# A fused pooled attention and mixture of attention experts: zero matmuls in groups of two, and a new order of all units

## The chip, the cores and the metric

The kernel runs on one core of a Trainium2 chip. The metric is device time in microseconds of one execution. The core has five engines with queues of their own: TensorE (PE, matrix products; PEld is its loading of the stationary operand), VectorE (DVE), ScalarE (ACT), GpSimd (POOL) and SyncE (SP, which here issues all DMA transfers). Each engine works through its own instructions in order and waits on semaphores for the others.

## The reference

Two stages, joined without a pause. With B = 8 batches, H = 8 heads, S = 576 rows, D = 64 columns and E = 4 experts:

```python
# stage 1: attention to keys and values averaged over windows of 8 rows
k_p = k.reshape(B, H, 72, 8, D).mean(axis=3)
v_p = v.reshape(B, H, 72, 8, D).mean(axis=3)
attn = softmax(q @ k_p.T / 8)                      # 576 x 72 for each head
x = (attn @ v_p).transpose(0, 2, 1, 3).reshape(B, S, 512)
# stage 2: each expert is a causal attention of one head; each row takes its two best
logits = x @ w_gate                                 # 4 per row
w = softmax of the two largest logits of a row
for e in range(4):
    a = softmax(causal((x @ wq[e]) @ (x @ wk[e]).T / 8))     # 576 x 576
    out += w[row, e] * (a @ (x @ wv[e]) @ wo[e])             # rows that chose e
```

The inputs q, k, v are 9.4 MB each in float32, the weights 2 MB together; the output is 9.4 MB.

## The kernel before

All matrix products are in bf16. A batch of 576 rows is cut into 512 main rows and 64 tail rows; the tails of two batches (b - 1 and b, for odd b) are put together and treated as one tile of 128 rows.

The work is cut into *units*, each a small Python generator that is run step by step. A unit's first step issues its TensorE work (or its load), the next step the evacuation of the PSUM tile by ScalarE or VectorE, a third step what follows. The string `ORDER` lists the steps of all units in the order in which they are issued: `2:kp` is the next step of unit `kp` of batch 2, `W:...` are units without a batch. `in_order` keeps each engine's instructions in the order in which they were issued, so `ORDER` fixes every engine's queue, the order of the loads on SP included. At the end of the kernel function a loop goes through it:

```python
for name in ORDER.split():
    if name not in parts:
        parts[name] = units[name]() or iter(())
    next(parts[name], None)
```

The units by name, for batch b:

- Loads, on SP: `lk`, `lq`, `lv` (1 MB each; in batch 0 halves `lka`, `lkb` and so on), the tails `lkt`, `lvt`, `lqt` (128 KB each), the weights `W:lq`, `W:lk`, `W:lv`, `W:lo`. All go through one DMA queue.
- `ks`, `vs`, `qc`: pairwise sums of the keys (ksum) and values (vsum), the cast of the queries (qbf), on GpSimd, for batch 0 on VectorE and ScalarE too. `kt`, `vt`, `qt`: the same for the tails (kts; vtp and vts; qtb).
- `kp`, `vp`: pooling by a matmul with a matrix of 1/8. `kp` is eight matmuls that read ksum and then four that read kts.
- `q0` to `q3`: transposes of the queries (qT). `s0` to `s3`: scores (sA), then the exponential on ScalarE (etA). `a0` to `a3`: attention times values (oA), then VectorE's division (x_tm). `x0` to `x3`: transposes of x (xT).
- `v0`, `v2`: the experts' values and the gate's logits (v_ps). `p0` to `p3`: the experts' queries and keys (p_ps), copied by ScalarE. `p0` and `p2` read wq, `p1` and `p3` read wk; `W:c0` to `W:c3` are ScalarE's casts of these weights. `g1` to `g6`: the gate on VectorE, GpSimd and ScalarE (g_lm, g_msk, g_w and so on).
- `c00`, `c01`, `c10`, `c11`, `c2`: the experts' scores in pieces (sB), exponential on ScalarE (etB, etC), GpSimd's causal mask. `o0`, `o1`: times values (oB). `t0`, `t1`: transposes (oT). `w0` to `w3`, `y0` to `y3`, `z0`, `z2`: output projection (y_ps), copy, store.
- For the pair of tails, under the odd batch: `qx`, `sx`, `ax`, `xx`, `pt`, `vx`, `h0`, `h1`, `hd`, `ox`, `tx`, `w4`, in the same sense.

The units `s*`, `c*`, `sx`, `h*` and `hd` have 64 rows in their contraction; all others have 72 or 128.

`W:h0` to `W:h9` are the function `busy`: four matmuls of 128x512 on a tile of zeros (`idle`, a view of `etd`), into a PSUM tile (idle_ps) that nobody reads. The tile comes from the pool `ps1`, which has two buffers and is shared with `q`, `x`, `t`, `kp`, `vp`, `p` and the `w` and `y` units; `s`, `a`, `v`, `c`, `o` and the like take turns in the three buffers of `ps2`.

Of the kernel before, what the change touches and what calls it, by code (L numbers as in the profile page):

```python
# [21 lines left out]
0:lkb 0:lqb 0:lkt W:h6 W:h9 0:lvb W:h5 0:qcb1 0:ksb W:h2 0:lqa 0:kt 0:lva 0:qcb0 0:qca0 W:h3 W:h8
0:qca1 0:lvt 0:q3 0:q3 0:q2 0:lka 0:vsb W:h0 1:lkt 0:vsa 0:kpb 1:kt 0:q2 0:q1 0:kpb 0:q1 0:q0 1:lk
0:ksa 0:s2 0:kpa 0:q0 0:vt 0:kpa 0:vp 0:s2 1:lq 0:s1 0:s3 1:ks 1:qc W:lv 1:lv 0:vp 0:a2 W:h4 0:s1
0:a1 W:lq 0:a2 0:s3 0:a3 0:s0 1:kp W:h1 0:a1 0:s0 0:a3 0:a0 W:h7 1:kp 1:lvt 1:q2 0:a0 1:q0 1:q2 1:q0
0:lqt 1:q3 1:q1 1:q3 1:vs 1:s2 1:lqt 1:q1 1:s3 0:x1 0:x1 1:vt W:cv 0:x2 1:s0 0:x3 0:x2 1:qt 0:x3
1:s2 1:s0 0:x0 1:s3 1:s1 0:x0 0:v2 0:v2 0:v0 1:vp W:lk W:c2 2:lq 0:v0 1:vp 0:p2 0:g1 1:s1 W:c0 2:lkt
0:p2 1:a1 0:g2 2:lvt 1:a3 1:qx 2:lk 1:a2 W:c3 0:p0 1:a1 1:qx 2:lv 1:a3 W:c1 0:g3 1:a0 1:a2 0:p3 0:p0
1:sx 0:g4 0:g5 2:qc 0:p1 1:a0 0:p3 1:sx 0:c11 3:lq 0:c10 1:x2 0:p1 3:lkt 1:x1 1:x2 0:c11 1:x1 2:lqt
0:c2 1:x0 1:x0 1:x3 0:c10 1:ax 1:x3 2:q3 3:lqt 2:q3 3:lk 1:p2 2:kt 0:g6 0:c11 0:c2 2:vt 3:lv 0:c00  # L30
0:c01 2:q2 1:p2 0:c2 2:q0 0:c10 2:ks 0:c01 1:ax 2:q2 1:v0 2:q1 4:lkt 2:q0 1:v0 1:xx 0:o1 1:v2 2:q1
0:c01 1:xx 3:lvt 2:kp 1:v2 0:c00 2:kp 1:pt 0:o1 2:s0 2:s2 2:vs 1:vx 1:pt 2:s0 0:c00 0:t1 1:vx 1:g1
2:s1 2:s3 2:vp 0:t1 1:g2 2:s2 0:o0 1:p0 2:s3 2:vp 2:s1 3:kt 2:a3 2:a1 0:o0 2:a2 1:p0 3:qt 1:p3 1:p3
1:p1 2:a3 4:lq 3:qc 4:lk 2:a2 2:a1 2:a0 1:p1 1:c10 3:qx 1:c10 3:q1 2:a0 3:q1 3:ks 1:h1 3:qx 1:hd
2:x3 2:x2 1:h1 2:x3 2:x2 1:h0 1:hd 2:x0 2:x1 2:x0 1:c11 1:c00 3:vs 3:vt 2:x1 1:c10 3:q0 3:q3 3:q0
1:g3 1:h0 2:v0 1:g4 3:q3 3:kp 1:c11 3:kp 1:c00 2:v2 0:t0 3:s3 2:v0 0:t0 1:c2 3:q2 2:v2 3:q2 2:p0
1:c2 4:kt 3:vp 3:sx 2:p0 1:c01 2:p1 2:g1 3:s3 3:sx 5:lq 1:c01 3:vp 3:a3 1:hd 2:p2 3:ax 2:p1 3:a3
1:g5 2:p2 3:s1 3:s0 4:qc 1:c2 3:ax 4:q0 4:q0 1:g6 4:lv 3:s1 1:ox 4:lvt 1:ox 4:q1 1:c00 4:q1 3:s0
3:s2 3:s2 2:c01 4:ks 2:g2 1:c01 2:c00 4:q2 4:q2 3:xx W:lo 3:xx 3:a1 4:lqt 2:c01 3:a1 4:kp 3:pt 4:kp
3:a2 3:a2 2:c00 5:lkt 4:q3 3:a0 3:pt 1:o0 5:lqt 4:s1 5:lvt 2:p3 4:q3 3:a0 1:c11 3:x0 4:s1 2:p3 4:s0  # L40
4:s0 4:s2 5:qc 3:x1 1:o0 5:lk 3:x0 3:x1 4:s3 4:s3 5:q2 4:vs 4:vt 5:q2 1:t0 1:o1 5:vt 3:x3 2:g3 1:t0
3:x3 2:c2 3:x2 4:vp 3:x2 6:lvt 4:vp 2:c2 3:p1 1:o1 3:v0 2:c00 4:s2 2:c01 6:lkt 3:v0 5:lv 3:p1 5:q3
1:t1 2:c10 3:h0 1:t1 W:co 4:a1 2:c10 3:p3 4:a0 5:qt 5:q3 5:kt 3:p3 3:p2 3:p2 4:a1 5:qx 4:a0 2:c11
4:a3 5:q1 5:qx 2:g4 3:p0 3:h0 5:q1 4:a2 2:c10 2:c11 2:g5 0:w1 4:a3 3:p0 7:lkt 4:a2 3:c10 3:c11 5:ks
0:w1 5:kp 3:c10 4:x0 4:x0 3:v2 3:c11 5:kp 4:x2 4:x2 0:w0 2:c11 6:lq 2:c2 0:w0 3:c2 3:v2 5:s1 5:vs
4:x3 3:c2 2:g6 4:x1 4:x3 4:x1 2:o0 3:vx 3:vx 5:s1 6:lv 2:o0 4:p2 6:qc 4:p2 0:w3 3:g1 0:w0 5:s2 6:vs
5:sx 3:hd 0:w3 5:q0 0:w3 5:q0 4:p1 5:s2 2:o1 5:vp 2:o1 5:vp 5:sx 4:v2 4:p1 3:c11 0:w2 4:v2 3:c10
3:hd 5:a2 1:w3 6:kt 5:a2 0:w2 5:s3 5:s0 2:t0 1:w3 5:ax 6:q1 2:t0 5:ax 4:p3 6:lk 0:w1 6:vt 7:lvt 5:s0
5:a0 7:kt 6:q1 5:a0 5:a1 3:g2 4:p3 4:p0 3:c2 5:xx 5:s3 3:h1 5:a1 4:p0 3:c00 2:t1 5:xx 5:a3 6:lqt
7:vt 2:t1 3:h1 5:pt 5:a3 3:c00 1:tx 6:ks 1:tx 3:hd 5:pt 4:c2 3:c01 7:lq 6:q0 6:q0 5:x2 4:c2 4:v0  # L50
3:c01 5:x3 5:x2 6:q3 5:x3 7:lk 4:c01 4:c00 6:q3 7:qc 4:c01 6:kp 6:vp 6:kp 6:vp 4:c00 1:w3 4:c2 2:w0
3:o1 4:v0 2:w0 5:x0 5:x1 5:x0 3:c00 6:s3 3:g3 6:s1 7:q2 5:x1 7:lv 6:s3 6:s1 4:g1 3:ox 7:lqt 3:g4
7:q2 5:p3 3:g5 6:a1 3:g6 5:p3 3:ox 0:w2 5:p2 7:ks 5:p2 4:c01 3:o1 6:a1 1:w4 4:g2 5:hd 6:s0 1:w4 5:hd
6:q2 6:q2 2:w0 6:s0 6:a3 7:kp 1:w4 7:kp 3:c01 7:q3 6:s2 7:q3 2:w2 6:s2 3:o0 1:w2 2:w2 6:a3 6:a0 1:w2
3:o0 6:a0 2:w1 6:a2 2:w1 5:p1 7:vs 1:w0 4:c11 2:w2 6:a2 5:p1 1:w0 7:s2 4:c11 7:s3 5:vx 7:qt 7:s3
7:vp 7:s2 5:vx 5:v0 6:x3 7:vp 6:x3 4:g3 4:c00 5:v0 6:x1 5:v2 6:x1 6:x0 4:c10 4:c10 4:c11 1:w2 7:q1
7:a2 6:x0 2:w3 7:q1 5:p0 1:w0 2:w3 1:w1 5:v2 7:a2 5:g1 5:p0 7:s1 4:g4 1:w1 5:h0 3:t1 4:c10 4:g5 6:x2
4:g6 3:t1 5:g2 4:o1 7:s1 6:x2 7:qx 7:qx 4:o1 5:hd 5:h0 6:p2 7:q0 7:q0 7:sx 5:h1 5:c10 3:t0 6:p2 5:g3
7:sx 3:t0 6:p0 5:h1 7:a1 6:p3 6:v2 5:c10 4:o0 6:p3 1:w1 6:p1 7:a1 5:c10 6:v2 6:p0 3:tx 5:g4 7:a3
7:s0 4:o0 5:g5 3:tx 5:c2 6:p1 7:s0 3:y1 3:w4 7:a3 2:w1 2:w3 3:y1 7:ax 5:c2 7:a0 7:ax 3:w4 3:w0 7:a0  # L60
6:v0 3:y1 3:w0 3:w3 5:c00 5:g6 3:w3 7:x2 6:v0 5:c2 5:c01 7:x1 7:x2 7:x3 3:w4 5:c11 5:c00 7:x1 6:c10
4:t0 7:x3 5:c01 4:t0 5:c00 6:g1 5:ox 3:w0 7:xx 6:c2 5:c11 6:g2 6:c10 5:c01 5:c11 7:xx 6:c00 6:c2
7:vx 5:ox 5:o0 6:g3 7:vx 4:t1 4:t1 7:x0 6:c00 5:o1 7:x0 6:c10 4:w2 4:w2 7:p1 7:v0 5:o1 4:w2 5:o0
3:w3 7:p1 7:p3 4:y0 7:v0 7:p3 6:c11 6:c01 4:y0 4:y1 5:tx 6:c11 7:v2 6:c2 5:tx 3:w2 6:c01 4:y1 6:g4
7:p2 7:v2 6:c11 3:w2 6:c01 6:g5 7:p2 7:p0 6:g6 7:g1 5:t0 7:p0 7:c11 7:c10 6:c00 7:c10 5:t1 5:t0
7:c10 4:w3 6:o1 3:w2 5:t1 4:w3 7:c11 6:o0 7:g2 4:y0 5:w4 7:pt 6:o1 5:w4 5:y2 7:g3 7:c01 7:pt 6:o0
7:g4 4:y1 5:y2 7:c01 6:t0 6:t0 7:c2 6:t1 7:c2 7:g5 7:c11 7:g6 6:t1 4:w3 7:c2 5:y0 7:c00 5:w4 5:y0
5:y1 7:c00 7:h1 6:y1 5:y2 7:c01 5:y1 6:y1 5:y0 5:y1 7:c00 7:o1 7:h1 6:y1 6:w0 6:w0 7:o0 6:w0 5:w3
7:o1 7:t1 7:h0 5:w3 7:o0 7:hd 7:hd 7:t1 7:t0 7:h0 6:y3 7:t0 5:w3 7:z2 6:y3 7:hd 7:ox 6:y3 6:w2 7:z2
7:z0 7:ox 6:w2 7:tx 6:w2 7:tx 7:z0 7:w4 7:w4 7:w4  # L70
"""


# [880 lines left out]
```

## Time and profile before

| | |
|---|---|
| runs shown, us | 178.42, 177.4, 179.2 (median 178.42) |
| the profiled execution, us | 179.14 |
| its span, first to last instruction, us | 177.4 |
| mean granted TensorE clock | 0.965 |
| TensorE busy | 164.7 us, 93% of the span |
| VectorE, ScalarE, GpSimd busy | 70%, 70%, 59% |
| read from and written to memory | 30.42 MB, 9.44 MB |
| matmuls on zeros | 40, in all 13.5 us busy |

Times within the profile count from the first instruction. In the timeline each row is a run of equal instructions: start, busy time, engine, line, operation, tiles, shapes, count, and in brackets the engine's idle time in front of it with what ended it. Nearly all instructions carry one line, L121, since a helper issues them; so they are told apart by tiles. A row for a stretch of time gives, after its length, the busy time of PE, PEld, DVE, ACT and POOL with their counts, then the granted clock, the DMA share and GB/s. In the row of the granted clock over 40 slices, 9 is full. Matmuls overlap at their ends, so that the time that a group of them takes is read from its start to the start of the next one.

### The profile page before, as it was taken

The page shows a single profiled execution, that of the slowest core. Times are in us where ns is not written, and L with a number is a line of the kernel's source. Part 1 is how long each engine was busy: PE and PEld are TensorE (multiplying, and loading weights), DVE is VectorE, ACT ScalarE, POOL GpSimd, SP SyncE. Part 2 cuts the span into 40 slices and gives each one's busy share as a digit, 9 for nine tenths or more (in the row PEclk, how much of TensorE's full clock was granted, in tenths as well). Part 3 has the DMA queues.
Part 4 walks back from the last instruction along what each step waited for, and adds up shares of the span by engine and source line. Part 5 has one row for each costly group of instructions (what it writes and reads, how often), then busy time and mean ns, then how long its engine had stood idle before and what let it go on. Part 6 is the DMA issues. An engine that isn't in the chain of part 4 may idle for free.

```text
span 177.4 us, 5397 instructions
## 1 busy us (share of the span) xinstructions
PE 164.7 (93%) x2172; PEld 105.3 (59%) x2172; DVE 124.2 (70%) x356; ACT 124.2 (70%) x172; POOL 103.9 (59%) x223
## 2 busy tenths in 40 slices
...
PEclk9978569999999999999999999999999999999997
DMA  4999999999799999799995999824040222165656
GB/s 154 314 313 308 346 304 200 337 276 312 185 259 328 305 336 343 168 240 270 276 318 133 321 318 361 235 61 177 6 181 0 91 92 76 46 236 164 256 183 234
DMA packets 38681, 40.20 MB, mean 227 GB/s; under 512 B 5632, under 2 KB 33792, under 8 KB 38656
## 3 DMA queue, kind: packets, MB, share of 16 engines
...
q8 instruction: 17, 0.28, 0.7%
...
HBM read 30.42 MB, written 9.44 MB: 225 GB/s over the span
## 4 chain that ended last, share of the span: by engine, by line
PE 68%; DMA 12%; SPq 7%; DVE 3%; ACT 3%; POOL 3%; issue 1%; DVEq 0%; POOLq 0%; ACTq 0%
PE p_ps L121 12%; PE v_ps L121 7%; SPq L121 7%; PE y_ps L121 7%; DMA ktail<-in_k_dram 5%; DMA qtail<-in_q_dram 5%; PE sB_ps L121 5%; PE oB_ps L121 4%; PE oA_ps L121 4%; PE sA_ps L121 4%; PE qT_ps L121 3%; PE xT_ps L121 3%; PE vp_ps L121 3%; PE idle_ps L121 2%; PE oBt_ps L121 2%; PE oT_ps L121 2%
## 5 line engine op out<-in xcount | busy, mean ns | idle before, releaser
L121 ACT ACTIVATE etA<-sA_ps 72x1024 bf16<-72x1024 f32 x32 | 31.6, 1020 | 14.2 <-PE sA_ps L121 13.9
L121 ACT ACTIVATE etB<-sB_ps 128x1024 bf16<-128x1024 f32 x32 | 31.8, 1031 | 2.8 <-PE sB_ps L121 2.3
L121 PE MATMUL p_ps<-xT,wqk 128*128 128x512 bf16 x128 | 32.6, 379 | 0.0
L121 POOL TENSOR_SCALAR_AFFINE_SELECT etB<-etB 128x256 bf16<-128x256 bf16 x48 | 18.6, 409 | 17.6 <-ACT etB L121 17.3
L121 ACT CAST qk<-p_ps 128x512 bf16<-128x512 f32 x32 | 18.6, 587 | 11.3 <-PE p_ps L121 11.2
L121 POOL TENSOR_TENSOR vsum<-vraw 128x512 bf16<-128x512 f32 (+1 forms) x16 | 18.9, 1203 | 9.8 <-DMA vraw<-in_v_dram 9.8
L121 DVE TENSOR_TENSOR x_tm<-oA_ps,rzA 128x512 bf16<-128x512 f32 x32 | 22.1, 692 | 1.1
L121 PEld LDWEIGHTS <-wqk 128*128 128x128 bf16 x192 | 14.6, 98 | 9.7 <-issue 0.4
L121 POOL TENSOR_TENSOR ksum<-kraw 128x512 bf16<-128x512 f32 x14 | 17.5, 1270 | 2.5 <-DMA kraw<-in_k_dram 2.5
L121 PE MATMUL y_ps<-wo_t,oT 128*128 128x512 bf16 x64 | 18.6, 380 | 0.0
L121 PE MATMUL v_ps<-wvg,xT 128*128 128x260 bf16 x128 | 16.8, 274 | 0.4 <-DVE xT L121 0.2
L121 PE MATMUL idle_ps<-etD 128*128 128x512 bf16 x40 | 13.5, 497 | 3.7 <-DVE qT L121 2.4
L121 DVE COPY xT<-xT_ps 128x512 bf16<-128x512 bf16 x32 | 12.6, 420 | 5.5 <-PE xT_ps L121 5.2
L121 DVE COPY qT<-qT_ps 128x512 bf16<-128x512 bf16 x32 | 13.1, 420 | 4.7 <-PE qT_ps L121 4.4
L121 ACT COPY ofin<-y_ps 128x512 f32<-128x512 f32 x20 | 11.7, 589 | 4.8 <-PE y_ps L121 3.5
L121 PEld LDWEIGHTS <-etA 72*128 72x128 bf16 x256 | 11.8, 102 | 5.3 <-issue 1.9
L121 POOL CAST qbf<-qraw 128x2048 bf16<-128x2048 f32 x7 | 13.2, 1892 | 1.4 <-DMA qraw<-in_q_dram 1.4
L121 PE MATMUL sB_ps<-qk 64*128 64x256 bf16 (+3 forms) x128 | 13.8, 300 | 0.0
L121 PEld LDWEIGHTS <-xT 128*128 128x128 bf16 x128 | 11.9, 97 | 3.2 <-DVE xT L121 0.5
L121 PE MATMUL oA_ps<-vp,etA 72*128 72x65 bf16 x256 | 13.3, 200 | 0.2 <-DVE vp L121 0.2
L121 PE MATMUL qT_ps<-ident,qbf 128*128 128x128 bf16 x128 | 12.1, 225 | 1.0 <-POOL qbf L121 0.6
L121 PEld LDWEIGHTS <-etB 128*128 128x128 bf16 x256 | 11.4, 97 | 1.6 <-POOL etB L121 0.2
(121 smaller groups left out, 331.7 us busy)
## 6 DMA issues: line engine op xcount, KB each, us to landing
...
```

The lines of the kernel that those rows point to most:

```text
L121: return tc.keep_in_program_order(fn(*args, **kwargs))
```

## The change

`busy` issues two matmuls in place of four, and there are 24 such units in place of ten, so 48 matmuls on zeros in place of 40. `ORDER` is another permutation: each other unit has as many steps as before.

```diff
     def busy():
         ps = ps1.tile([128, 512], FP32, name="idle_ps", tag="ps1")
-        for _ in range(4):
+        for _ in range(2):
             pe.matmul(out=ps[:], lhsT=idle[:, 0:128], rhs=idle, start=True, stop=True)
 
-    for n in range(10):
+    for n in range(24):
         units[f"W:h{n}"] = busy
```

`ORDER` has some fifty lines on either side; the sequences that follow from it on single engines are these. TensorE, the beginning (a unit stands where its TensorE work is issued; h is one group on zeros):

```text
before  h h h h h h 0:q3 0:q2 h 0:kpb 0:q1 0:q0 0:s2 0:kpa 0:vp 0:s1 0:s3 0:a2 h 0:a1 0:a3 0:s0
        1:kp h 0:a0 h 1:q2 1:q0 1:q3 1:q1 1:s2 1:s3 0:x1 0:x2 1:s0 0:x3 0:x0 1:s1 0:v2 0:v0 1:vp
        0:p2 1:a1 1:a3 1:qx 1:a2 0:p0 1:a0 0:p3
after   h h h h h h h 0:q1 h h h 0:q0 0:q3 h h 0:kpb h h 0:s3 0:kpa 0:q2 0:s0 0:s1 h h h 0:vp
        0:s2 h h 0:a0 0:a1 h 0:a2 1:kp 0:a3 h h h 1:q3 h 0:x0 1:s3 0:x1 1:q0 0:x2 0:x3 1:s0 1:q1
        0:v2 0:v0 1:q2 1:s1 1:s2 1:vp 0:p2 1:a3 1:a1 1:qx 1:a0 0:p0 1:a2 0:p3
```

TensorE, from there to the experts' first work on batch 2:

```text
before  1:sx 0:p1 0:c11 0:c10 1:x2 1:x1 0:c2 1:x0 1:x3 1:ax 2:q3 1:p2 0:c00 0:c01 2:q2 2:q0 1:v0
        2:q1 1:xx 0:o1 1:v2 2:kp 1:pt 2:s0 2:s2 1:vx 0:t1 2:s1 2:s3 2:vp 0:o0 1:p0 2:a3 2:a1 2:a2
        1:p3 1:p1 2:a0 1:c10 3:qx 3:q1 1:h1 1:hd 2:x3 2:x2 1:h0 2:x0 2:x1 1:c11 1:c00 3:q0 3:q3
        2:v0 3:kp 2:v2 0:t0 3:s3 1:c2 3:q2 2:p0 3:vp
after   1:sx 0:p1 1:x0 0:c10 0:c11 1:x3 1:x2 1:ax 0:c01 2:q0 1:x1 0:c00 0:c2 1:p2 1:xx 1:v0 2:q1
        2:q2 1:v2 2:kp 2:q3 0:o1 2:s0 1:pt 1:vx 2:s1 2:s3 2:s2 0:t1 2:vp 0:o0 1:p0 2:a0 2:a2 1:p3
        2:a1 1:p1 2:a3 3:qx 1:hd 1:h1 3:q1 1:c10 1:c00 2:x0 2:x1 1:h0 2:x3 2:x2 1:c11 3:kp 3:q3
        2:v0 3:q0 3:q2 1:c2 3:s3 2:v2 2:p0 0:t0 1:c01 3:sx 3:s1 3:vp
```

TensorE, the end:

```text
before  ... 6:o0 5:w4 7:pt 5:y2 7:c01 6:t0 7:c2 6:t1 5:y0 7:c00 5:y1 7:h1 6:y1 7:o1 6:w0 7:o0
        5:w3 7:t1 7:h0 7:hd 7:t0 6:y3 7:z2 7:ox 6:w2 7:z0 7:tx 7:w4
after   ... 5:w4 6:o0 5:y2 7:pt 7:c2 7:c00 6:t1 6:t0 7:c01 5:y0 5:y1 7:h1 6:y1 7:o1 6:w0 7:o0
        5:w3 7:t1 7:h0 7:hd 7:t0 6:y3 7:z2 7:ox 6:w2 7:z0 7:tx 7:w4
```

The loads on SP, the first 29 and 30:

```text
before  0:lkb 0:lqb 0:lkt 0:lvb 0:lqa 0:lva 0:lvt 0:lka 1:lkt 1:lk 1:lq W:lv 1:lv W:lq 1:lvt 0:lqt
        1:lqt W:lk 2:lq 2:lkt 2:lvt 2:lk 2:lv 3:lq 3:lkt 2:lqt 3:lqt 3:lk 3:lv
after   0:lvt 0:lqa 0:lkb 0:lqb 0:lkt 0:lka 0:lvb 0:lva 1:lkt 1:lk 1:lq W:lv 1:lvt 1:lv W:lq 1:lqt
        2:lkt 0:lqt W:lk 2:lq 2:lvt 2:lk 2:lv 3:lkt 3:lq 3:lqt 2:lqt 3:lk 3:lv 3:lvt
```

GpSimd, around batches 2 and 3 (masks named by their tile):

```text
before  ... ksum2 etB vsum2 etB g_lm g_msk kts3 qtb qbf3 ksum3 vsum3 vtp3 vts3 etB g_w ...
after   ... ksum2 etC etB g_G vsum2 etB qtb qbf3 g_lm g_msk ksum3 kts3 g_w g_d g_den etD vsum3 vtp3 vts3 ...
```

More of the change, by code (lines that the diff above doesn't have):

```diff
@@ L21 @@
 ORDER = """
[L22 to L70, printed above, removed]
+W:h21 W:h19 0:lvt W:h11 W:h12 0:lqa 0:qca1 0:lkb 0:lqb W:h16 0:lkt W:h1 W:h0 0:qca0 0:ksb 0:q1 W:h23
@@ new lines @@
+0:p2 W:c3 1:qt 1:a1 W:c1 1:qx 1:a3 1:qx 1:a0 0:p0 0:g2 1:a2 1:a0 2:lk 0:g3 0:p3 0:p0 0:p3 1:a1 0:g4
+2:lv 1:sx 2:qc 1:sx 0:p1 1:a2 3:lkt 1:x0 1:x0 0:p1 0:g5 0:c10 3:lq 0:c11 0:c10 2:vt 3:lqt 1:x3 1:x2
+1:ax 1:x3 0:c01 2:q0 0:c11 1:x2 1:x1 2:lqt 0:c10 1:ax 3:lk 0:c00 0:c11 0:c2 1:x1 1:p2 2:ks 0:c01
+2:q0 0:c2 1:xx 1:p2 0:c00 1:xx 1:v0 0:c2 0:c01 0:g6 2:q1 2:q2 2:q1 1:v2 2:q2 2:kp 2:q3 2:vs 1:v0
+2:kp 0:c00 0:o1 3:lv 2:q3 0:o1 2:s0 4:lvt 1:v2 1:pt 2:s0 1:vx 2:s1 1:vx 2:s3 2:s2 1:pt 1:g1 0:t1
+2:s1 2:vp 0:o0 0:t1 2:vp 2:s2 3:qt 2:s3 3:qc 1:p0 2:a0 2:a2 1:p3 0:o0 1:p0 2:a1 1:p1 2:a0 3:lvt 2:a2
@@ new lines @@
+1:p3 1:g2 2:a3 3:ks 3:qx 1:p1 4:lq 1:hd 2:a1 2:a3 1:h1 3:kt 1:g3 3:q1 1:hd 3:q1 3:qx 1:c10 1:g4
+1:c00 1:h1 2:x0 2:x0 1:hd 2:x1 1:h0 2:x3 1:c10 3:vs 3:vt 2:x1 1:c00 2:x2 1:c11 2:x3 3:kp 2:x2 3:kp
+3:q3 1:g5 2:v0 3:q0 3:q3 4:qc 1:c11 4:lk 3:q2 1:h0 4:lkt 2:v0 1:c2 3:s3 3:q0 2:v2 3:q2 2:p0 0:t0
+2:v2 5:lq 4:ks 1:c2 1:c01 0:t0 3:s3 3:sx 4:kt 4:lv 3:s1 2:p0 1:g6 4:vt 3:vp 3:vp 2:p2 1:c01 4:q0
+3:sx 3:a3 4:q0 2:g1 1:c00 3:s1 3:ax W:lo 2:p2 2:p1 4:q1 3:s0 3:a3 1:c2 2:p1 3:s0 3:s2 4:q1 3:ax 5:lk
+4:q2 1:ox 2:c00 2:c01 4:q2 1:c01 3:s2 5:lkt 2:c00 1:ox 5:qc 3:xx 3:a1 4:kp 3:a2 3:xx 1:c11 2:c01
```

37 lines of the change are left out of this document (added).

## The prediction

> **What bounds the kernel now.** I read the page first: span, granted clock and DMA in 40 slices.
>
> ```profile
> span 177.4 us, 5397 instructions
> ...
> PEclk9978569999999999999999999999999999999997
> DMA  4999999999799999799995999824040222165656
> ```
>
> The reader is to see that DMA is at its limit nearly throughout for 25 of the 40 slices (4.4 us each, to 111 us), and that the clock is below full only in slices 3 to 6. So there is a first regime in which loads come too late for TensorE, and a second in which TensorE alone is the bound. The chain of waits, in order of time, says where the first one ends:
>
> ```profile
> 34.22 1.04 ACT wqk L121 x2
> ...
> 44.12 8.79 DMA qtail<-in_q_dram
> ```
>
> This transfer, on the chain until 52.9 us, is the last load in it. So what TensorE does before that time is not worth its own length: it counts only by how much work is left when the last late transfer has been digested. GpSimd digests the loads; its timeline gives their arrivals, since an idle time that ended with a DMA ends at the landing:
>
> ```profile
> 21.73 1.89 POOL L121 CAST qbf<-qraw 128x2048 bf16<-128x2048 f32 x1 [0.51 <-DMA qraw<-in_q_dram]
> ...
> 43.24 2.50 POOL L121 TENSOR_TENSOR ksum<-kraw 128x512 bf16<-128x512 f32 x2 [0.67 <-DMA kraw<-in_k_dram]
> ...
> 49.56 0.22 POOL L121 TENSOR_TENSOR g_lm<-L,g_mx 128x20 f32<-128x20 f32 x1
> ...
> 51.55 0.46 POOL L121 TENSOR_TENSOR kts<-ktail 128x128 bf16<-128x128 f32 x1 [1.23 <-PE p_ps L121]
> 53.06 0.61 POOL L121 CAST qtb<-qtail 128x512 bf16<-128x512 f32 x1 [1.05 <-DMA qtail<-in_q_dram]
> 53.62 1.90 POOL L121 CAST qbf<-qraw 128x2048 bf16<-128x2048 f32 x1
> 55.79 2.52 POOL L121 TENSOR_TENSOR ksum<-kraw 128x512 bf16<-128x512 f32 x2 [0.27 <-DMA kraw<-in_k_dram]
> ```
>
> TensorE's own timeline, around the places that the change touches:
>
> ```profile
> 24.78 1.16 PE L121 MATMUL idle_ps<-etD 128*128 128x512 bf16 x4
> 25.78 0.61 PE L121 MATMUL qT_ps<-ident,qbf 128*128 128x128 bf16 x8
> ...
> 35.58 1.03 PE L121 MATMUL p_ps<-xT,wqk 128*128 128x512 bf16 x4
> ...
> 45.80 0.38 PE L121 MATMUL kpT_ps<-pm,ksum 128*128 128x64 bf16 x7 [0.21 <-POOL ksum L121]
> ...
> 54.53 0.40 PE L121 MATMUL qTt_ps<-ident,qtb 128*128 128x128 bf16 x4
> 55.57 0.40 PE L121 MATMUL qT_ps<-ident,qbf 128*128 128x128 bf16 x4 [0.64 <-POOL qbf L121]
> ...
> 58.58 0.62 PE L121 MATMUL qT_ps<-ident,qbf 128*128 128x128 bf16 x8
> 59.38 1.05 PE L121 MATMUL v_ps<-wvg,xT 128*128 128x260 bf16 x8 [0.17 <-ACT etX L121]
> 60.27 0.39 PE L121 MATMUL kpT_ps<-pm,ksum 128*128 128x64 bf16 x8
> 60.50 0.26 PE L121 MATMUL kpT_ps<-pm,kts 128*128 128x32 bf16 x4
> 60.61 1.05 PE L121 MATMUL v_ps<-wvg,xT 128*128 128x260 bf16 x8
> 61.50 0.38 PE L121 MATMUL oT_ps<-ident,o_sc 128*128 128x128 bf16 x4
> 61.82 0.39 PE L121 MATMUL sA_ps<-qT,kp 64*128 64x512 bf16 x2
> 62.04 0.38 PE L121 MATMUL sB_ps<-qk 64*128 64x256 bf16 x4
> 62.36 0.40 PE L121 MATMUL qT_ps<-ident,qbf 128*128 128x128 bf16 x4
> 62.59 0.59 PE L121 MATMUL p_ps<-xT,wqk 128*128 128x512 bf16 x2
> ```
>
> Matmuls overlap, so I take times from start to start. The row of 45.80 is 2:kp, waiting for batch 2's key sums; that of 55.57 is 3:q1, waiting for GpSimd's cast; both are the DMA regime showing through.
>
> **The change part by part.**
>
> *Eight more zero matmuls (48 for 40).* Four at half clock run from 24.78 to 25.78, partly after the clock has recovered, so about 0.25 us each; at half clock throughout it would be near 0.4 us. All 48 stand ahead of batch 0's value projection 0:v2, in the loading regime. Cost if uncovered: 8 x 0.25 = 2.0 us (0.2 to 0.4 each: 1.6 to 3.2). What covers them: TensorE waits for loads there anyway. I take zero.
>
> *The start.* Before, batch 1's queries are cast by 21.73 + 1.89 = 23.6, but TensorE begins them at 25.78 because zero groups of four stand in front. After, batch 0's attention outputs stand ahead of 1:kp, and three groups of two between 0:a3 and 1:q3. 1:kp needs GpSimd's ksum, done by 21.2 (GpSimd is idle for 0.51 us before 21.73) and, now behind it, kts (0.46, row of 51.55): 21.7. Then 0:a3 and six zero matmuls (1.5 to 2.4) lead to 1:q3 at 23.6 to 24.4, 1.4 to 2.2 us sooner. That doesn't hold: 0:p3 needs wk, whose cast on ScalarE (34.22, two casts in 1.04) released it at 35.58, and in the new load order batch 2's key tail stands in front of wk. That is a small transfer; I put wk at the old time to 1 us later. So 0:p3 comes between 34.8 and 35.9, against 35.58. I take no change.
>
> *2:kp.* The loads issued up to batch 2's keys are the same set in both orders (counted in ORDER), and DMA is at its limit throughout, so they land again at 43.2 and ksum ends at 43.24 + 2.50 = 45.7. The new order runs 2:kp before 2:q3 and 0:o1, which stood ahead of it: 0.22 + 0.61 = 0.83 us of work that is no longer done by then. TensorE waits here, and loses up to 0.83 us for the moment.
>
> *3:q1.* The transfers up to the later q tail of batches 2 and 3 are again the same set; it lands at 53.0, the cast ends at 53.62 + 1.90 = 55.5. Before, TensorE stood at 3:qx at 54.53 and waited 0.64 us and more; the 0.83 us of moved work now fills that wait. So 3:q1 at about 55.6 as before: the loss is given back.
>
> *3:kp.* This is where the new order decides. It moves 3:kp ahead of 3:q3, 2:v0 and 3:q0, and on GpSimd moves batch 3's key tail (kts) from before the casts (51.55) to behind ksum, with three small gate steps (0.22 each, 0.7) in front of ksum. Its bound: 55.5 + 0.7 + 2.52 + 0.46 = 59.2. Before the end of 3:kp the new order has done just what the old one had done by 58.58 (3:q0), and 3:kp itself, which is 12 small matmuls, 0.34 us (60.27 to 60.61). So it is late by 59.2 - (58.58 + 0.34) = 0.28 us. TensorE arrives sooner: from 55.57 to 58.58 the old order ran 3.0 us of small units; the new one has h1 and hd (55.57 to 58.58 holds them, 0.6 us) already behind it and 1:c10 (0.2) still to do, so 2.6 us, and 3:kp begins near 58.2. It waits some 0.8 us between its first eight and its last four matmuls. Without the wait it would end at 58.5 and be ahead by 0.4 us; with GpSimd 0.5 us later than reckoned, behind by 0.8. I take +0.28, from the row of the wait's releaser.
>
> *2:v0.* Before, it started 0.8 us after 3:q0 for 0.45 us of transposes, so it lost 0.33 us to late copies of xT. After, its transposes are older by a whole 3:kp. -0.33.
>
> *Switches between 64-row and 128-row work.* In the last four rows: oT before a 64-row unit takes 0.32 us (61.50 to 61.82), qT before other 128-row work 0.23 (62.36 to the next unit at 62.59); sA before another 64-row unit takes 0.22, sB before a 128-row unit 0.32. Each stretch of 64-row units thus costs 0.2 us. Counted in ORDER there were 52 such stretches, now 49; the three that go lie behind 2:v0, where nothing but TensorE is the bound. -0.6 us. It could be nothing if other waits fill the holes, and I see no way in which it costs.
>
> *The rest.* Every unit is there once in both; behind 60 us the new order permutes neighbours. The last eighteen units of TensorE, from 5:y1 to 7:w4, stand in the same sequence, and so do the stores. Tail: 0, bounded by 0.5 us either way from the order of 7:c01 and 7:c00 in front of it.
>
> Sum: 0.28 - 0.33 - 0.6 = -0.65 us. The profiled execution took 179.14 us, its span 177.4 us; the runs shown have a median of 178.42 us, 0.7 us under it. So 178.5 us against the profiled execution, and **177.8 us** as a median.
>
> **The clock.** The wait in 3:kp has a second price. Three stretches of 3.41 us at the start:
>
> ```profile
> 14.82:18.24 3.41, 2.13 (x22) 1.14 (x23) 1.94 (x5) 1.21 (x2) 1.20 (x3) 1.00 1.09 330
> 18.24:21.65 3.41, 3.20 (x30) 2.01 (x29) 1.45 (x5) 1.73 (x2) 2.49 (x2) 0.50 1.10 346
> 21.65:25.07 3.41, 3.41 (x27) 1.72 (x28) 1.74 (x5) 2.14 (x3) 1.89 (x1) 0.50 1.10 346
> ```
>
> In the first TensorE was busy for 2.13 of 3.41 us, 62%, and the granted clock (the column before the DMA share) was 0.50 in the next two. The Trainium skill, "TensorE: Matmul & The Clock Gate", Part 1 and the closing table, says that the clock falls after a whole idle window of some 3.4 us and tells the author to avoid gaps over about 3 us. By that rule a wait of 0.8 us would cost nothing beyond itself; the first row disagrees, as no gap there was near 3 us, and the measurement decides.
>
> **The rivals.**
>
> *Slower: the clock drops in the middle of the kernel.* Place: the wait in 3:kp (or that in 2:kp). It decides if the idle time in one window passes about 1.3 us (38% of 3.41, as in the first row). One window at half clock costs 1.7 us, two as in the trace 3.4 us: 179.5 to 181.2 us. For it: 0.8 us of expected idle time, and as much in front of it at 2:kp, are not far off. Against it: in a wait that falls across two windows neither is idle enough, and between 25 and 175 us the clock never fell in the trace of before, with the wait at 55 us in it. Chance 0.18. To the same side, at 0.08: the extra zero matmuls are not covered (0:p3 later than 36.5), 179.4 to 181 us.
>
> *Faster: the loading regime ends sooner.* If the later q tail and batch 3's keys land 1.5 us sooner, 3:q1 and the bound of 3:kp move by as much: 178.42 - 0.65 - 1.5 = 176.3 us. For it: the chain of before has a DMA on it as late as 52.9 us. Against: the same bytes stand in front of each late transfer, and DMA had no idle time to give. Chance 0.22.
>
> *The change does nothing:* the start is taken back and the switches fill other waits, 178.4 us. It lies inside the forecast's own range.
>
> **How the numbers follow.** The forecast, with its own range of 176.6 to 179.4 us (from the wait in 3:kp gone and the tail 0.5 us better, to the switches at nothing, that wait 0.5 us longer and the tail 0.5 worse), has 0.52. I call 1% (1.8 us) the least that a measurement tells from no change: faster is under 176.6, slower over 180.2. The faster rival lies mostly under its bound and a little of the forecast's lower side with it: 0.23. The slower ones at 0.26 lie mostly over theirs: 0.20. Within 1%: 0.57. The range that leaves out one in ten on each side is 175.9 to 180.5 us.
>
> **What would show it.** In the profile of the changed kernel: 0:p3 at 34.8 to 35.9; ksum of batch 2 again released by its DMA near 43.2 and 2:kp waiting for it; 3:q1 near 55.6 without a wait over 0.3 us; an idle time of about 0.8 us within 3:kp, ended by kts; granted clock 1.00 from 30 us on. If 2:kp or 3:kp come more than 1 us sooner, the claim that the same set of loads lands at the same time is wrong; if the clock falls after 30 us, the slower rival is right; if TensorE's work from 3:kp to the end isn't about 0.6 us shorter, the price of the switches is.

## The result and the profile after

| | before | after |
|---|---|---|
| time, us, median of 20 executions each | 178.43 (177.28 to 180.56) | 179.76 (178.53 to 181.51) |
| ratio to before | | 1.0071 [1.0042, 1.0099] |
| profiled execution, us, and its span | 179.14, 177.4 | 180.0, 178.3 |
| mean granted TensorE clock | 0.965 | 0.992 |
| TensorE busy | 164.7 us, 93% | 163.3 us, 92% |

The change costs 1.3 us where I forecast a gain of 0.65 us. The time is within 1% of before and within the range of 175.9 to 180.5 us, but it is on the other side of before, and outside the forecast's own 176.6 to 179.4 us. Ratios compare means without the few executions that lie over 1.5% above the fastest of their kernel, while medians are of all; two traces below, that without zeros and that of the late moves on GpSimd, are of such executions, and only their landings, their durations in the start and their wait at one place are read. The page of the changed kernel:

```profile
span 178.3 us, 5414 instructions
...
PEclk9999999999999999999999999999999999999996
DMA  3999998999999999969998997124050050443766
```

The clock row is full to the last slice, where before it fell in four slices. DMA is again at its limit for about 25 slices. So TensorE had, by this row, a better clock, it had less busy time, and it was later all the same: it waited more. The chain of waits, in order of time, has the later tails of the queries on it as before, and a stretch that before's did not need:

```profile
44.05 9.23 DMA qtail<-in_q_dram
...
105.95 1.28 POOL vsum L122
107.64 1.84 POOL qbf L122
```

GpSimd is on the chain at 106 to 109 us, 50 us behind the place where I had let the loading regime end. What TensorE waited for after 60 us, first before, then after (columns: waiting and releasing engine with tile, us in all, times, longest):

```profile
PE yt_ps L121 <- DVE oTt L121: 0.4, 1, 0.4
PE oT_ps L121 <- DVE o_sc L121: 0.2, 1, 0.2
```

```profile
PE oB_ps L122 <- POOL etB L122: 0.6, 1, 0.6
PE yt_ps L122 <- DVE oTt L122: 0.4, 1, 0.4
PE p_ps L122 <- ACT qk L122: 0.2, 1, 0.2
PE oT_ps L122 <- DVE o_sc L122: 0.2, 1, 0.2
```

Two waits are new: one of 0.6 us for a mask of GpSimd, one of 0.2 us for a copy of ScalarE. The first on TensorE, at 3:o1, and what GpSimd did before it:

```profile
109.97 0.60 PE L122 MATMUL y_ps<-wo_t,oT 128*128 128x512 bf16 x2
111.17 0.33 PE L122 MATMUL oB_ps<-vaug,etB 128*128 128x65 bf16 x5 [0.60 <-POOL etB L122]
```

```profile
100.25 2.50 POOL L122 TENSOR_TENSOR ksum<-kraw 128x512 bf16<-128x512 f32 x2 [1.95 <-DMA kraw<-in_k_dram]
...
104.72 2.50 POOL L122 TENSOR_TENSOR vsum<-vraw 128x512 bf16<-128x512 f32 x2
107.18 0.46 POOL L122 TENSOR_TENSOR kts<-ktail 128x128 bf16<-128x128 f32 x1
107.58 1.90 POOL L122 CAST qbf<-qraw 128x2048 bf16<-128x2048 f32 x1
109.43 0.77 POOL L122 TENSOR_SCALAR_AFFINE_SELECT etB<-etB 128x256 bf16<-128x256 bf16 x2
110.14 0.62 POOL L122 CAST qtb<-qtail 128x512 bf16<-128x512 f32 x1
110.70 0.77 POOL L122 TENSOR_SCALAR_AFFINE_SELECT etB<-etB 128x256 bf16<-128x256 bf16 x2
```

The reader is to see a chain without a hole: batch 6's keys land at 100.18, GpSimd sums them from 100.25 and works on to the masks of 3:c11 (109.43) and 3:c10 (the first of the two at 110.70), which 3:o1 needs. Their exponentials had long been done; in `ORDER` the masks stand behind the cast of batch 7's queries. In the kernel before the same three masks were done by 98.6 us, 11 us ahead of 3:o1, and 3:o1 started 0.43 us behind 2:w0 (y_ps), where the changed kernel has 1.20 us:

```profile
97.44 1.13 POOL L121 TENSOR_SCALAR_AFFINE_SELECT etB<-etB 128x256 bf16<-128x256 bf16 x3
```

```profile
109.19 0.59 PE L121 MATMUL y_ps<-wo_t,oT 128*128 128x512 bf16 x2
109.62 0.31 PE L121 MATMUL oB_ps<-vaug,etB 128*128 128x65 bf16 x5
```

To place the loss I use TensorE's *lag*: how much later it starts a unit than the kernel before had come to the same amount of work, both counted from the first instruction, matmuls on zeros left out. It is exact where both orders have done the same units; elsewhere it depends by some 0.2 us on how long each unit is taken to be. At such places the changed kernel is 0.70 us late (63.5 us of the kernel before), then 0.78 (106 us), 1.50 (118 us) and 1.59 (170 us). The jump is 3:o1.

### The profile page after: what moved, and what is told of

Same layout as the page of the kernel before. It is cut to its first block, busy times and chain, and to the rows that moved or that the text cites. A ratio compares the mean times of both kernels' runs of the same rounds, so it can differ in the third digit from the quotient of the medians.

```text
span 178.3 us, 5414 instructions
## 1 busy us (share of the span) xinstructions
PE 163.3 (92%) x2180; PEld 104.9 (59%) x2180; DVE 123.8 (69%) x356; ACT 124.6 (70%) x172; POOL 103.2 (58%) x223
## 4 chain that ended last, share of the span: by engine, by line
PE 50%; DMA 18%; SPq 10%; POOL 7%; ACT 5%; DVE 4%; issue 3%; DVEq 0%; POOLq 0%
PE p_ps L122 11%; SPq L122 10%; DMA qraw<-in_q_dram 7%; PE y_ps L122 6%; PE v_ps L122 6%; DMA qtail<-in_q_dram 5%; DMA wk_f<-in_moe_wk_dram 5%; PE oB_ps L122 4%; PE sB_ps L122 3%; POOL qbf L122 3%; PE sA_ps L122 3%; PE oA_ps L122 2%; PE oBt_ps L122 2%; PE xT_ps L122 2%; PE qT_ps L122 2%
## 5 line engine op out<-in xcount | busy, mean ns | idle before, releaser
L122 PE MATMUL idle_ps<-etD 128*128 128x512 bf16 x48 | 14.3, 422 | 4.2 <-DVE qT L122 2.2
L122 PE MATMUL sB_ps<-qk 64*128 64x512 bf16 (+3 forms) x128 | 13.5, 300 | 0.5 <-ACT etD L122 0.4
L122 PE MATMUL oB_ps<-vaug,etB 128*128 128x65 bf16 x256 | 12.4, 193 | 0.6 <-POOL etB L122 0.6
L122 PEld LDWEIGHTS <-etA 72*128 72x128 bf16 x256 | 10.6, 97 | 3.6 <-DVE vaug L122 0.2
```

Of the source, the lines that this page charges most:

```text
L122: return tc.keep_in_program_order(fn(*args, **kwargs))
```

## The experiments

Each is compared with the kernel before on the same chip; the ratio has its 95% interval. Where a diff shows `ORDER`, only the moved steps and their neighbours stand in it.

**1. The suspected masks alone.**

```diff
-... 3:h1 5:a3 4:c2 7:qc 1:tx 3:c01 3:c11 5:x2 7:qt ... 6:vp 3:c10 3:c00 ...
+... 3:h1 5:a3 4:c2 3:c11 3:c10 7:qc 1:tx 3:c01 5:x2 7:qt ... 6:vp 3:c00 ...
```

> The changed kernel with one difference: GpSimd's masks for 3:c11 and 3:c10 stand ahead of its cast of batch 7's queries (7:qc, 1.90 us), not behind that cast and the copy 7:qt. Theory (the order of GpSimd's queue costs 0.77 us at 3:o1): TensorE no longer waits at 3:o1 near 110 us, its work after that comes 0.6 to 0.8 us sooner, and the time is about 179.0 us, 0.35 to 0.45% under the changed kernel. Rival (another wait fills the hole, or the cast of batch 7's queries is then late for 7:q2): the time stays at 179.7 us.

Measured: 179.46 us, 1.0073 [1.0047, 1.0098]. TensorE no longer waits at 3:o1, but in the profiled execution it was 1.29 us late at 106 us already, so it had little to wait for. By time the theory fails here; experiments 9 and 10 come back to it.

**2. Two early tail loads put back**, and with them the GpSimd steps that read them, 1:vt and 2:kt.

```diff
-W:lv 1:lvt 1:lv ... W:lq W:h6 ... 1:lqt 2:lkt 1:qc 1:vt ... 2:lq W:h17 ... 2:kt 2:lvt ... 2:qc 1:sx
+W:lv 1:lv ... W:lq 1:lvt W:h6 ... 1:lqt 1:qc ... 2:lq 2:lkt W:h17 ... 1:vt ... 2:lvt ... 2:qc 2:kt 1:sx
```

> The changed kernel with two of the small tail loads put back where the kernel before had them: batch 2's key tail behind batch 2's queries, batch 1's value tail behind wq. Theory (in the loading regime everything that TensorE waits for comes late by the small loads in front of it, but batch 2's keys end the regime and have the same loads in front of them in all orders): wk and batch 2's queries land 1 to 2 us sooner than 35.0 and 39.2 us, 2:q0 loses its wait of 0.72 us, but 2:kp and 3:kp stay within 0.3 us of 45.8 and 59.4, so the time falls by no more than 0.5 us. Rival (the late loads at the start are what makes the changed kernel slower): the time falls by 1.0 to 1.3 us, to that of the kernel before.

Measured: 179.86 us, 1.0086 [1.0061, 1.0111]. wk and batch 2's queries landed at 34.2 and 37.7 us, 0.8 and 1.6 us sooner, and the lag at 36.5 us went from 0.50 to nothing. At 63.5 us it was 1.18: batch 3's keys landed at 56.6 us (56.1 in the changed kernel). What the start gains is not carried past those keys.

**3. The start and the rest exchanged.**

```diff
-ORDER: all of one kernel
+ORDER: one kernel's steps up to 1:a2 (or 1:sx) near 37 us, then the other's order for what is left
```

> The start of the changed kernel, all 24 groups of two matmuls on zeros and its loads included, up to the second half of 1:a2 near 37 us, and from there the order of the kernel before. Theory (the start costs little, since 2:kp and 3:kp wait for the same loads; the loss comes later): 178.4 to 178.9 us, as the kernel before. Rival (the eight more matmuls on zeros and the late wk make the loss): 179.5 to 179.8 us, as the changed kernel.

> The mirror of the run before: the start of the kernel before, with its ten groups of four matmuls on zeros and its loads, up to the first half of 1:sx near 37 us, and from there the order of the changed kernel. Theory (the loss comes after the start): 179.4 to 179.8 us, as the changed kernel. Rival (the loss is made in the start): 178.3 to 178.6 us, as the kernel before.

Measured: new start and old rest 178.24 us, 1.0006 [0.9973, 1.0039]; old start and new rest 179.08 us, 1.0053 [1.0013, 1.0093]. The new start, with its 48 matmuls on zeros, was 0.75 us late at 42 us and 0.19 us early from 58 us to the end. The loss lies behind 37 us.

**4. The same cut near 79 us.**

```diff
-ORDER: all of one kernel
+ORDER: one kernel's steps up to 5:q2 near 79 us, then the other's order for what is left
```

> The changed kernel up to 5:q2 near 79 us, and from there the order of the kernel before. Theory (half of the loss lies behind 80 us, in TensorE's waits for GpSimd's masks at 3:o1 and for PSUM tiles to be emptied, which took the place of the stretches of 64 rows that are gone): 178.8 to 179.2 us, and the time from the landing of batch 3's keys to the end of TensorE's work as in the kernel before plus 0.3 us. Rival (all of it lies in the loading regime, where loads land later): 179.5 to 179.8 us, as the changed kernel.

> The mirror: the kernel before up to 5:q2 near 79 us, with its ten groups of four matmuls on zeros, and from there the order of the changed kernel. Theory (half of the loss lies behind 80 us): 178.7 to 179.1 us, and the time from the landing of batch 3's keys to the end of TensorE's work 0.3 to 0.8 us longer than in the kernel before. Rival (all of it lies in the loading regime): 178.2 us, as the kernel before.

Measured: new order to 79 us and old behind it 178.88 us, 1.0041 [1.0011, 1.0071]; the mirror 180.16 us, 1.0121 [1.0075, 1.0167]. The mirror is not clean: its order asks for 5:kp sooner than the old loads bring batch 5's keys (82.3 us, 80.3 in the changed kernel), and TensorE waits 1.0 us there for GpSimd. But it has the same moral: an order of TensorE's units is only as good as the loads and the GpSimd queue that it was made with. And the first of the two has the old masks and no wait at 3:o1, and is still 0.1 to 0.7% slower than before: a part of the loss lies ahead of 79 us.

**5. No matmuls on zeros, and half as many again.**

```diff
-... W:h21 W:h19 0:lvt W:h11 W:h12 0:lqa ...
+... 0:lvt 0:lqa ...
```

```diff
-        for _ in range(2):
+        for _ in range(3):
             pe.matmul(out=ps[:], lhsT=idle[:, 0:128], rhs=idle, start=True, stop=True)
```

> The changed kernel with no matmuls on zeros at all; nothing else differs. Theory (their time is covered by waits for loads, and they keep the granted clock up in the start): TensorE is busy 14 us less, the granted clock falls to about half in the start, and the time is the same within 0.5 us if the loading regime covers that too, up to 1.5 us longer if it doesn't. Rival (the matmuls on zeros are on the path, 48 at 0.2 us and more): the time falls by over 1 us, to 178.6 us or less.

> The changed kernel with three matmuls on zeros in each of the 24 groups, so 72 for 48; nothing else differs. The 24 more take 24 x 0.22 = 5.3 us of TensorE at full clock, of which 14 x 0.22 = 3.1 us stand in front of the first queries; between 5 and 25 us TensorE was idle for 4.9 us in the profile of the changed kernel. Theory (covered): batch 0 and 1 come up to 2 us later at 25 us, but 2:kp and 3:kp wait for the same loads, so the time is the same within 0.5 us. Rival (on the path): up to 5 us longer.

Measured: without them 180.65 us, 1.0128 [1.0071, 1.0186]; with 72 of them 180.36 us, 1.0134 [1.0078, 1.019]. In the trace of the second the 24 more were covered: the lag was 0.86 us at 36.5 us and nothing at 63.5 us, under that of the changed kernel. Then TensorE came to 3:o1 early and waited 1.21 us for the same masks: lag 0.34 at 106 us, 1.45 at 110.5. By time the expectation of at most 0.5 us is missed: the ratio is 0.6% over the 1.0071 of the changed kernel, though the intervals overlap. Its trace loses another 0.65 us between 121 and 129 us, where a matmul of 7:vp waits 0.29 us for a copy of ScalarE; why, no run shows. The kernel without them is told of in the last section.

**6. GpSimd's order in the middle.**

```diff
-2:vp 2:s2 3:qt 2:s3 3:qc ... 1:g2 2:a3 3:ks 3:qx ... 1:h1 3:kt 1:g3
+2:vp 2:s2 3:qc 3:qt 2:s3 ... 1:g2 2:a3 3:kt 3:ks 3:qx ... 1:h1 1:g3
```

> The changed kernel with two moves on GpSimd: the cast of batch 3's queries (3:qc) stands ahead of the cast of the later query tails (3:qt), and batch 3's key tail (3:kt) ahead of its key sums (3:ks). In the profile of the changed kernel GpSimd waited 3.36 us, to 53.43, for the tails, though the queries had landed at 51.7, and ended the key tail at 59.48. Theory (the order of GpSimd's queue makes 3:q1 and 3:kp late): 3:q1 waits no more, 3:kp ends 0.5 us and more sooner against the landing of batch 3's keys, and the time is 0.3 to 0.7 us under the changed kernel, 179.0 to 179.4 us. Rival (TensorE gives it back at a later wait): 179.7 us.

Measured: 179.81 us, 1.0068 [1.0035, 1.01]. It did what it was made for: at 63.5 us TensorE was 0.54 us *ahead* of the kernel before. Two waits took it all: right behind that TensorE fell back by some 0.7 us (4:q0 waited 0.67 us for batch 4's queries, which landed at 64.0 us, 63.9 in the kernel before), and at 3:o1 it waited 2.1 us for the masks. Lag 0.01 at 106 us, 1.98 at 110.5.

**7. One copy of ScalarE.** ScalarE around 64 us in the changed kernel, and TensorE's 2:p1:

```profile
64.03 0.58 ACT L122 CAST qk<-p_ps 128x512 bf16<-128x512 f32 x1 [0.21 <-PE p_ps L122]
64.58 1.02 ACT L122 ACTIVATE etB<-sB_ps 128x1024 bf16<-128x1024 f32 x1
65.50 1.01 ACT L122 ACTIVATE etT<-sAt_ps 72x1024 bf16<-72x1024 f32 x1
66.41 1.02 ACT L122 ACTIVATE etA<-sA_ps 72x1024 bf16<-72x1024 f32 x1
67.31 0.58 ACT L122 CAST qk<-p_ps 128x512 bf16<-128x512 f32 x1
```

```profile
67.95 1.02 PE L122 MATMUL p_ps<-xT,wqk 128*128 128x512 bf16 x4 [0.23 <-ACT qk L122]
```

Three exponentials follow each other, from the units 1:c01, 3:sx and 3:s1, which the new order puts side by side. The copy that frees the PSUM tile for 2:p1 comes behind them.

```diff
-... 4:q0 2:g1 1:c00 3:s1 3:ax W:lo 2:p2 2:p1 ...
+... 4:q0 2:g1 1:c00 2:p2 3:s1 3:ax W:lo 2:p1 ...
```

> The changed kernel with one move on ScalarE: the copy of 2:p2's result stands ahead of the exponential of 3:s1. In the profile of the changed kernel three units of 64 rows stood side by side there, ScalarE worked without a hole from 64.03 to 67.89 us, and 2:p1 came 0.39 us late, for want of the PSUM tile which that copy empties. Theory (units of 64 rows side by side save TensorE a switch, but send ScalarE an exponential of 1.0 us for every 0.23 us of TensorE, and the wait for ScalarE takes the saving back): the wait at 2:p1 is gone, TensorE stands 0.3 to 0.4 us better at 70 us against the landing of batch 3's keys, and keeps it to the end; 179.4 us. Rival (3:a1 or 4:kp then waits): the same work is as late as before by 74 us, and the time stays at 179.7 us.

Measured: 179.64 us, 1.0103 [1.006, 1.0145]. The copy now starts at 66.59 and 2:p1 at 67.43, right behind 3:ax, and between 63.5 and 70.8 us the lag falls from 0.57 to 0.30, where in the changed kernel it rose from 0.70 to 0.81: 0.38 us better. At 106 us it was 0.27, at 110.5 1.27. After 60 us TensorE waited for:

```profile
PE oB_ps L122 <- POOL etB L122: 1.1, 1, 1.1
PE yt_ps L122 <- DVE oTt L122: 0.4, 1, 0.4
PE y_ps L122 <- DVE oT L122: 0.2, 1, 0.2
PE oT_ps L122 <- DVE o_sc L122: 0.2, 1, 0.2
```

The wait for ScalarE is gone, and the one at 3:o1 has grown in its place.

**8. All late moves on GpSimd, and all moves together.**

```diff
-... 1:t0 3:p1 5:qt ... 3:p3 3:p2 5:kt 2:c10 ...
+... 1:t0 3:p1 5:kt 5:qt ... 3:p3 3:p2 2:c10 ...
```

This, with the masks of experiment 1, is the first; the second adds experiments 6 and 7.

> The changed kernel with three moves on GpSimd behind 80 us: the masks of 3:c11 and 3:c10 ahead of the cast of batch 7's queries, and batch 5's key tail (5:kt) ahead of the cast of the query tails (5:qt). Theory (GpSimd's queue, fed by loads that land at a time of their own, sets the earliest time of 5:kp and 3:o1, so a TensorE that comes sooner only waits there: 0.60 us in the profile of the changed kernel, 1.21 us in that with three matmuls on zeros): no wait of TensorE for GpSimd is left behind 80 us, and the time is 0.4 to 0.8 us under the changed kernel, 178.9 to 179.3 us. Rival (in most executions TensorE comes later than those masks anyway, and the wait belongs to the profiled one): 179.5 to 179.8 us.

> The changed kernel with the moves of the three runs before together. Theory (the three waits add up, and they are what the changed kernel lost): 178.0 to 178.6 us, no slower than the kernel before by more than 0.2%. Rival (they hide each other, or the landing of the loads alone sets the time): 179.0 us and more.

Measured: 178.80 us, 1.0016 [0.9989, 1.0044], and 178.75 us, 1.0032 [1.0005, 1.006]. Neither trace has a wait for a mask at 3:o1. The loss is gone but for 0.2 to 0.3%; the moves in the middle add nothing to the late ones that these times show.

**9. Key tail or masks; the late masks put into the kernel before.** The first kernel has the move of 5:kt from experiment 8 alone, the third that of the masks alone again. The second is the kernel before with

```diff
-... 3:c11 ... 3:c10 ... 1:w3 4:c2 2:w0 3:o1 4:v0 ...
+... 1:w3 4:c2 2:w0 3:c11 3:c10 3:o1 4:v0 ...
```

> The changed kernel with one of the three late moves alone: batch 5's key tail (5:kt) ahead of the cast of the query tails (5:qt). Theory (3:o1's masks make the loss, this move nothing): TensorE still waits at 3:o1 for GpSimd, and the time is that of the changed kernel, 179.5 to 179.8 us. Rival (the late key tail makes 5:kp late in most executions): 178.7 to 179.0 us, as with all three moves.

> The kernel before with the suspected cost put in: GpSimd's masks for 3:c11 and 3:c10 moved from 97.4 us to behind the cast of batch 7's queries and the masks of 4:c01, 4:c00 and 4:c2, just ahead of 3:o1's own place; nothing else differs. There they end at about 108.9 + 1.2 + 1.1 = 111.2 us, and 3:o1 started at 109.62 in the profile of the kernel before. Theory (3:o1 waits for its masks, and nothing behind gives it back): a wait of 1.3 to 1.6 us for GpSimd at 3:o1, and 179.5 to 179.9 us. Rival (the wait is given back behind it, or the order of GpSimd's queue hardly counts): under 178.7 us.

> The first experiment once more, beside the key tail alone on the same chip: the changed kernel with the masks of 3:c11 and 3:c10 ahead of the cast of batch 7's queries. Theory (the masks alone make the late loss): 178.7 to 179.1 us, as with all three late moves, and the first time was high because loads landed late in its few executions. Rival (the masks don't matter): 179.5 us and more, as the first time.

> The three late moves on GpSimd and the copy of 2:p2 ahead of the exponential of 3:s1, without the moves in the middle. Theory (what TensorE gains at 2:p1 was only swallowed at 3:o1, and shows once that wait is gone): no wait of TensorE over 0.3 us between 80 us and 165 us, 0.2 to 0.4 us better than the late moves alone, 178.4 to 178.6 us. Rival (a later load takes it): 178.8 us, as the late moves alone.

Measured: the key tail alone 179.22 us, 1.0061 [1.0031, 1.009]; late masks in the kernel before 180.33 us, 1.0076 [1.0042, 1.011]; the masks moved ahead, alone, 178.41 us, 1.0003 [0.9978, 1.0029]; late moves and copy 178.35 us, 1.001 [0.9985, 1.0035]. All four ran on one chip, and the intervals of the key tail alone and of the masks alone don't overlap. The kernel before with late masks, on GpSimd and on TensorE:

```profile
107.04 1.89 POOL L121 CAST qbf<-qraw 128x2048 bf16<-128x2048 f32 x1 [0.29 <-DMA qraw<-in_q_dram]
108.89 0.77 POOL L121 TENSOR_SCALAR_AFFINE_SELECT etC<-etC 128x256 bf16<-128x256 bf16 x2
109.61 1.49 POOL L121 TENSOR_SCALAR_AFFINE_SELECT etB<-etB 128x256 bf16<-128x256 bf16 x4
```

```profile
110.79 0.33 PE L121 MATMUL oB_ps<-vaug,etB 128*128 128x65 bf16 x5 [1.24 <-POOL etB L121]
```

Its lag is -0.23 us at 106 us, 1.12 at 118 and 1.40 at 170: 1.35 us lost at 3:o1, and nothing behind it gives it back. The changed kernel with the masks ahead, in the same two views:

```profile
99.92 2.50 POOL L122 TENSOR_TENSOR ksum<-kraw 128x512 bf16<-128x512 f32 x2 [2.29 <-DMA kraw<-in_k_dram]
...
107.26 1.12 POOL L122 TENSOR_SCALAR_AFFINE_SELECT etB<-etB 128x256 bf16<-128x256 bf16 x3
108.34 1.89 POOL L122 CAST qbf<-qraw 128x2048 bf16<-128x2048 f32 x1
```

```profile
110.03 0.31 PE L122 MATMUL oB_ps<-vaug,etB 128*128 128x65 bf16 x5
```

The masks end at 108.38, and 3:o1 starts at 110.03 without a wait.

**10. The changed kernel and the masks ahead, side by side.**

> The changed kernel itself, beside the masks alone on the same chip. Theory (TensorE waits at 3:o1 for the late masks in most executions): 0.5% to 0.9% over the kernel before, 179.2 to 180.0 us, and slower than the masks alone by 0.6 us and more. Rival (the masks' place counts for nothing, and the two times of the masks alone differ by the chip): the same time as the masks alone within 0.3 us, whatever it is.

> The masks of 3:c11 and 3:c10 ahead of the cast of batch 7's queries, a third time, beside the changed kernel on the same chip. Theory: within 0.3% of the kernel before, 0.6 us and more under the changed kernel. Rival: as the changed kernel within 0.3 us.

Measured: the changed kernel 179.17 us, 1.003 [0.9997, 1.0062]; the masks ahead 178.69 us, 1.0018 [0.9988, 1.0048]. The difference of 0.48 us has the theory's sign but not the 0.6 us and more that were expected, and the intervals overlap, so this pair alone shows nothing. In the trace of the changed kernel, its fastest execution (178.42 us), batch 6's keys landed at 98.62 us, not at 100.18; the mask of 3:c10 ended by 109.6, 3:o1 started at 109.60, and 0.23 us was lost there.

**The runs together.** There are ten traces in which the late part has the changed order with its late masks. In nine of them 3:o1 starts 10.98 to 11.00 us after batch 6's keys landed, though they landed anywhere between 97.9 and 101.9 us: there the landing and GpSimd's queue behind it set the time, and TensorE doesn't. (In the tenth, the mirror of experiment 4, it is 11.73 us, behind TensorE's own work.) Where nothing holds it, 3:o1 starts 0.43 us behind 2:w0, so that the loss can be read in each: from nothing to 2.05 us, 0.77 us on the mean of the ten. Each trace with the masks ahead, or with the old order there, has the 0.43 us. The executions of the changed kernel from both measurements (31) average 179.5 us, those of the masks ahead from all three (30) 178.7 us. What stays open is why the first measurement of the masks ahead, six executions on another chip, gave 179.46 us: its one trace shows loads that landed some 0.9 us later than in the second's, and no wait at 3:o1. No version beat the kernel before.

## Why the prediction was wrong

The step that failed is the last of the sum: "behind 60 us the new order permutes neighbours", put at 0, with its ground in the reading of the profile, a second regime "in which TensorE alone is the bound". The new order moved two masks behind loads' work in GpSimd's queue. That gave 3:o1 an earliest time of its own, 11.0 us after batch 6's keys land, and TensorE comes there within some 2 us of that time. So the price is a maximum, not a sum: 0.77 us in the profiled execution and on the mean of the traces, 2.05 us where TensorE came early. I compared the queues of GpSimd around batches 2 and 3 only. The second step that failed is the one in front of it, the -0.6 us for switches: behind 60 us nothing of it showed, and 0.38 us was lost instead at a copy of ScalarE. The loss then adds up, by an estimate from the traces. With the landing of batch 3's keys taken out (55.72 us before, 56.05 after), TensorE at 74 us is 0.49 to 0.58 us later than in the kernel before in all ten traces that have the changed order up to there; with the 0.77 us of 3:o1 that makes 1.3 us.

The other steps, with the rows of the changed kernel, first GpSimd, then TensorE:

```profile
53.43 0.61 POOL L122 CAST qtb<-qtail 128x512 bf16<-128x512 f32 x1 [3.36 <-DMA qtail<-in_q_dram]
53.98 1.89 POOL L122 CAST qbf<-qraw 128x2048 bf16<-128x2048 f32 x1
...
56.56 2.50 POOL L122 TENSOR_TENSOR ksum<-kraw 128x512 bf16<-128x512 f32 x2
59.03 0.45 POOL L122 TENSOR_TENSOR kts<-ktail 128x128 bf16<-128x128 f32 x1
```

```profile
36.08 1.03 PE L122 MATMUL p_ps<-xT,wqk 128*128 128x512 bf16 x4
...
45.78 0.40 PE L122 MATMUL kpT_ps<-pm,ksum 128*128 128x64 bf16 x8
...
55.93 0.40 PE L122 MATMUL qT_ps<-ident,qbf 128*128 128x128 bf16 x4 [0.41 <-POOL qbf L122]
...
57.03 0.39 PE L122 MATMUL sB_ps<-qk 64*128 64x512 bf16 x2 [0.38 <-ACT etD L122]
...
59.35 0.39 PE L122 MATMUL kpT_ps<-pm,ksum 128*128 128x64 bf16 x8
59.58 0.26 PE L122 MATMUL kpT_ps<-pm,kts 128*128 128x32 bf16 x4
59.68 0.38 PE L122 MATMUL qT_ps<-ident,qbf 128*128 128x128 bf16 x4
59.91 1.06 PE L122 MATMUL v_ps<-wvg,xT 128*128 128x260 bf16 x8
```

- *Zeros at no cost:* right. The new start with the old rest is as fast as before, and in the trace with 24 more TensorE had made up for them by 63.5 us.
- *The start:* 0:p3 at 36.08, just past my 34.8 to 35.9. wk landed 1.7 us later than before (34.98 for 33.24) where I had allowed 1 us, and experiment 2 shows that it doesn't matter.
- *2:kp and 3:q1:* right in time. 2:kp came at 45.78 on the same landing (43.0 us, before 43.2), but behind TensorE's own work, not with the wait that I had forecast; 3:q1 came at 55.93 for 55.6, and its wait of 0.41 us is just over the 0.3 that I had allowed.
- *3:kp:* its bound came at 59.48 (59.03 + 0.45) for 59.2, as the tails of the queries, behind which the chain hangs, landed 0.4 us later than before. With that taken out, TensorE was some 0.4 us late behind 3:kp, for the 0.28 of the sum: the size was right, in part by luck. The idle time of 0.8 us within it did not show, since 3:q1 and a wait of 0.38 us at 57.03 held TensorE back first, and 3:kp began at 59.35 for 58.2. That GpSimd's queue did bind there is shown by experiment 6.
- *2:v0:* right. Across it the lag falls by some 0.35 us, for the 0.33 forecast.
- *Switches, -0.6 us:* wrong. Behind 60 us there are 33 stretches of 64-row units for 36, but from start to start, over the shortest unit of each kind, one costs 0.227 us for 0.209: 7.5 us both times. With the masks ahead, so without the wait at 3:o1, the lag still rises by 0.20 to 0.24 us from 63.5 to 170 us in the three traces that have them alone, where it should have fallen by 0.6. Shown of this are the 0.38 us at 2:p1, where units side by side, 0.23 us of TensorE each, send ScalarE an exponential of 1.0 us each: with the landing of batch 3's keys taken out, the two traces with that copy moved alone (experiments 7 and, with the late moves, 9) are 0.11 and 0.12 us late at 74 us, for the 0.49 to 0.58 of the ten others. In the times this gain is not clear of noise. Whether the other savings went the same way is not shown.
- *The clock:* the slower rival was wrong: the granted clock reads full from the start to 175 us, and four matmuls of the experts' queries and keys take 1.03 us at 36.08 as at 35.58 before. Its condition isn't borne out either. From 6.83 to 10.24 us TensorE was busy for 1.18 of 3.41 us, far under the 62% behind which I had let the clock fall; the granted clock stayed at 1.00, and four transposes at 10.16 took 0.39 us, as they do later on. The faster rival was wrong too: the tails of the queries and batch 3's keys landed 0.4 and 0.3 us later, not 1.5 sooner.
